# Attention and MLP-mixer kernel: halved fp32 first loads, earlier crossbar transposes, other ring sizes and a new written order

## Chip, cores and metric

The kernel runs on one core of one Trainium2 chip. The metric is device microseconds of one execution; less is better. The time of the kernel before is the median of three runs.

## What is computed

Squared-ReLU attention over 8 batches of 12 heads, 448 positions and 64 channels, and on its result an MLP mixer with a token part and a channel part. Inputs and output are fp32; the kernel computes in bf16 with fp32 sums.

```python
def _attn_ref(q, k, v):                      # 8 x 12 x 448 x 64
    scores = np.matmul(q, k.transpose(0, 1, 3, 2)) / np.sqrt(64)
    attn = np.maximum(scores, 0.0) ** 2 / 448
    return np.matmul(attn, v)

def _moe_ref(x, w_tok1, w_tok2, w_ch1, w_ch2):   # x: 8 x 448 x 768, heads side by side
    h = np.maximum(x.transpose(0, 2, 1) @ w_tok1, 0.0) @ w_tok2     # 448 -> 256 -> 448
    u = x + h.transpose(0, 2, 1)
    return u + np.maximum(u @ w_ch1, 0.0) @ w_ch2                   # 768 -> 1536 -> 768
```

## The kernel before, in words

The attention runs in 24 steps of four heads (three steps for a batch). A step `s` consists of these entries, whose names appear in the written order:

- `ldk`, `ldq`, `ldv`: loads by POOL's queue, which turn fp32 into bf16 on the way. Four buffers each for k and q, three for v. The very first q comes by SP's queue in fp32 (`ldf`) and is turned into bf16 by two `cast` entries.
- `T`: matmul transposes of k and q (56 of 64x64) into a bank, `cp`: copies of the two halves into `kqT`, one of three buffers. From step `QDMA` on the crossbar does this: `ik` and `iq` copy k and q into the only `side` buffer, `xk` and `xq` are DMA transposes on SP's queue from there to `kqT`.
- `S s.c`, c from 0 to 6: scores of 64 keys per head (four 64x64 matmuls of 448 columns), `r`: ReLU of the two banks into an `sq` buffer, on ACT (`:A`) or DVE (`:D`); `q s.c`: the square, on DVE. The `sq` buffers form a ring.
- `V s.c`: the product with v, summed over c; `xe`: eviction into `xT`.
- `X` and `xc`: transpose of x by matmuls and its copy; from step `XDMA` on `xd`, a DMA transpose on SP's queue, stands in their place.
- `t1`, `rt`, `t2`, `u`: the two token products, the ReLU between them, and u = x + h on DVE. `ub`: DMA transposes of u, by batch and 128 channels, into `u_sb`.

The channel part works on rows of 448 positions (one batch). Channel 1: batches 0 and 1 by plain products (`C1`, eviction `c1e`), the others by a scheme with seven products of blocks instead of eight (`Q1` to `Q7`, an entry is 6 matmuls of 224 columns; `m1` to `m4` and `y1` to `y4` are its sums of inputs and weights; `na`, `nb`, `nc` save interim sums; `h11` to `h22` write the result to `r2`). Channel 2 takes pairs of 128-row tiles, again with seven products (`P1` to `P7`, each of six matmuls of 384 columns; `s1` to `s4` and `ws` are the sums), `a`, `b`, `c` and `f11` to `f22` add u and write `out_sb`, `st` stores it. `r2` and `u_sb` are rings of `RING` slots of 128 rows: a channel 1 write waits for the P that read its slot. At `RING` = 8 a batch of 448 rows can lie across the end of the ring, and its write is then split in two.

The order of all entries on all engines is written out in one string, `ORDER`, with a bank number or an engine behind each name; each engine works its own entries strictly in that order. `fill:b*n` puts n matmuls without use on PE.

Of the kernel before, what the change touches and what calls it, by code (L numbers as in the profile page):

```python
# [7 lines left out]
FP32 = mybir.dt.float32  # L8
# [3 lines left out]
XDMA, QDMA = (8, 12)  # L12
# [3 lines left out]
RING = 8  # L16
# [46 lines left out]
ldf ldk0 ldq1 ldk1 ldv0 ident cast0:A cast1:D ldq2 T0.0:0 ldk2 T0.1:1 cp0.0:A ldv1 cp0.1:D ldv2 fill:2*7 S0.0:23  # L63
S0.1:45 S0.3:67 r0.0.0:A r0.0.1:D S0.6:01 ldk3 r0.1.1:A r0.1.0:D S0.4:23 r0.3.1:A ldq3 r0.3.0:D S0.5:54 r0.6.1:A
q0.1:D ldk4 S0.2:76 r0.5.1:A q0.0:D r0.2.1:A fill:1*5 T1.0:14 ldq4 r0.2.0:A r0.6.0:D r0.5.0:A cp1.1:D wt1.0 cp1.0:A
q0.2:D q0.3:D r0.4.1:A fill:6*25 S1.2:67 S1.0:05 r0.4.0:A q0.5:D V0.0:41 wt1.1 r1.0.1:A V0.1 r1.0.0:D V0.2 r1.2.0:A
q0.4:D V0.3 r1.2.1:A wt2 S1.4:32 q0.6:D S1.6:50 V0.4 r1.4.1:A S1.1:67 q1.0:D V0.5 r1.4.0:A r1.1.0:D r1.1.1:A S1.5:23
q1.2:D r1.6.1:A T2.0:67 r1.5.0:A q1.1:D V0.6 r1.5.1:A cp2.1:D ldv3 xe0.1:A cp2.0:D xe0.0:A ldq5 q1.4:D r1.6.0:A
fill:0*22 S2.0:02 S1.3:37 q1.5:D r2.0.1:A X0.0:1 ldk5 V1.0:64 r1.3.1:A r1.3.0:D V1.1 r2.0.0:A q1.6:D X0.1:5 xc0.0:A
S2.1:27 V1.2 q1.3:D S2.3:30 r2.1.0:A r2.1.1:D r2.3.1:A fill:1*6 S2.4:12 V1.3 q2.0:D r2.3.0:A V1.4 r2.4.1:A q2.1:D  # L70
T3.0:70 r2.4.0:A V1.5 q2.3:D cp3.1:A V1.6 cp3.0:D ldv4 q2.4:D xe1.0:A fill:1*9 S3.1:32 S2.5:17 xe1.1:A wc1.0.3
xc0.1:D V2.0:06 r2.5.0:D r2.5.1:A V2.1 S2.2:54 r3.1.1:A wc1.0.1 r3.1.0:D S3.2:71 r2.2.1:A r2.2.0:D T4.0:23 r3.2.1:A
wc1.0.0 q2.5:D S2.6:45 r3.2.0:A X1.1:1 q2.2:D r2.6.1:A wc1.0.2 r2.6.0:A cp4.1:D V2.2 S3.3:75 cp4.0:A xc1.1:D ldk6
V2.3 S3.0:43 r3.3.0:D V2.4 r3.3.1:A ldq6 t1.1.1:1 q2.6:D r3.0.1:A V2.5 q3.3:D r3.0.0:A V2.6 q3.1:D S3.4:27 rt1.1:A
S3.5:53 ldv5 xe2.1:A X1.0:4 xe2.0:D t1.0.1:1 r3.5.1:A wc1.1.1 xc1.0:D t2.1.1:6 r3.5.0:A rt0.1:D t1.0.0:0 r3.4.1:A
q3.0:D wc1.1.2 X2.1:3 r3.4.0:A t2.0.1:4 q3.2:D rt0.0:A S3.6:51 u0.1:D xc2.1:A X2.0:7 T5.0:20 r3.6.1:A r3.6.0:D
wc1.1.0 xc2.0:A V3.0:34 q3.4:D V3.1 cp5.0:A S4.2:15 q3.5:D V3.2 q3.6:D V3.3 r4.2.1:A wc1.1.3 t2.0.0:7 u1.1:D
# [20 lines left out]
C1.1.2:3 q8.1:D xe7.0:A ldk11 xe7.1:A q8.5:D t2.6.1:7 c1e1.2:A ldq11 S9.0:65 u6.1:D V8.1 S8.6:21 r9.0.1:A ldq13 V8.2
r9.0.0:D S9.1:37 r8.6.0:A C1.1.8:5 r8.6.1:D r9.1.1:A ldk13 q9.0:D r9.1.0:A q8.6:D V8.3 ub0.3 c1e1.8:A S9.5:62 V8.4
q9.1:D S9.3:17 V8.5 r9.5.1:A r9.5.0:D S9.4:35 V8.6 r9.3.1:A ub0.4 r9.3.0:D t2.6.0:2 xe8.0:A C1.0.0a:6 q9.5:D xe8.1:A  # L100
r9.4.0:A q9.3:D ub0.1 X7.0:7 r9.4.1:A C1.1.6:1 u6.0:D xc7.0:A q9.4:D ub0.5 ws3.1:D T10.0:40 c1e1.6:A S9.2:35 ws1.1:D
S9.6:27 cp10.1:A ub0.0 C1.1.7:1 r9.2.1:D r9.2.0:A r9.6.1:D r9.6.0:A ub0.2 C1.0.0 q9.2:D cp10.0:A C1.1.11:0 q9.6:D
c1e0.0:A xk12 c1e1.7:D V9.0:53 c1e1.11:A S10.1:72 ws2.1:D V9.1 S10.0:46 r10.1.0:A V9.2 xq12 r10.1.1:D S10.2:10
r10.0.0:A C1.0.8:7 ws4.1:D r10.2.0:A r10.2.1:A xd8 r10.0.1:D t1.7.0:2 c1e0.8:A q10.2:D q10.0:D ub1.0 S10.3:41
rt7.0:A V9.3 q10.1:D S10.5:06 r10.3.0:A V9.4 r10.3.1:D V9.5 r10.5.1:A V10.0:72 ub1.3 s1.0:D V9.6 r10.5.0:A V10.1
T11.0:41 q10.3:D xe9.0:A S10.4:60 xe9.1:A q10.5:D ub1.4 ldk15 C1.1.5:5 cp11.0:A cp11.1:D ldv11 r10.4.1:D r10.4.0:A
V10.2 s2.0:D c1e1.5:A S10.6:31 V10.3 S11.2:40 q10.4:D r10.6.0:A P1.0:6 r10.6.1:A ik13:D r11.2.1:A q10.6:D C1.1.0:5
# [12 lines left out]
r12.0.0:D r12.0.1:A r12.3.0:D nb.2.1:A P2.2:1 q12.0:D c.2:D Q7.2.1 f11.2:D P4.2 xd11 q12.3:D nc.2.1:A iq15:A f22.2:D  # L120
Q5.2.1:2 f21.2:D Q4.2.1 h22.2.1:D st5.0 P3.2 h21.2.1:A xk15 Q2.2.1:5 f12.2:D ub3.1 Q3.2.1 h11.2.1:D S13.0:34
# [710 lines left out]
```

## Time and profile before

| | |
|---|---|
| time, median of 3 runs | 351.92 us (351.30 to 352.77) |
| time of the profiled execution | 351.25 us |
| its span | 349.4 us |
| PE (matmul) busy | 339.6 us, 97% |
| DVE busy | 313.3 us, 90% |
| ACT busy | 223.3 us, 64% |
| POOL busy | 61.8 us, 18% |
| DMA moved | 48.78 MB, mean 140 GB/s |

Busy times come from start and end of instructions, with matmul ends modelled: rows of one engine overlap, so the step from one start to the next, not the length of a row, tells how fast an engine works. `[1.62 <-DMA kq_raw<-in_k_dram]` behind a row means that the engine had stood idle for 1.62 us and that this DMA ended the wait. In the windows, "17.50, 16.75 (x443)" is the length of the stretch, then PE's busy time and its instructions, then the other engines in the order that the heading gives; DMA share is the mean over 16 engines and can exceed 1 where transfers of two queues overlap.

### The profile page before, as it was taken

What the parts mean: (1) busy time and instruction counts of PE and PEld (TensorE: products, weight loads), DVE (VectorE), ACT (ScalarE), POOL (GpSimd) and SP (SyncE); (2) the same over time, 40 slices, a digit from 0 to 9 for tenths busy, and PEclk for the clock granted to TensorE, in tenths of its full rate; (3) what the DMA queues carried; (4) which work ended last, traced back from release to release, by engine and by line L of the source; (5) the groups of instructions that cost most, each with busy time, mean ns of one, the idle gap of its engine ahead of it and who ended that gap; (6) DMA issues with size and microseconds to landing.
All of it is one profiled execution on the core that took longest, in us unless ns stands there. A gap on an engine that the chain in (4) does not pass through costs nothing.

```text
span 349.4 us, 9700 instructions
## 1 busy us (share of the span) xinstructions
PE 339.6 (97%) x3964; PEld 220.0 (63%) x3964; DVE 313.3 (90%) x613; ACT 223.3 (64%) x443; POOL 61.8 (18%) x92
## 2 busy tenths in 40 slices
PE   6999999999999999999999999999999999999993
PEld 2666556555555577668765566666776677888662
DVE  1999999999999997999999999999999985687772
ACT  3999999799995474787655888778655222323100
POOL 8446424044011340004201112101000000000000
PEclk9999999999999999999999999999999999999998
DMA  8999979699999999899986989859853532633235
GB/s 141 201 163 173 208 116 174 114 166 145 150 166 143 192 189 185 139 159 155 187 179 110 195 133 174 168 93 127 145 118 67 104 87 57 127 67 81 57 92 135
DMA packets 93597, 48.78 MB, mean 140 GB/s; under 512 B 68016, under 2 KB 90224, under 8 KB 93552
## 3 DMA queue, kind: packets, MB, share of 16 engines
q1 hardware_dynamic: 68624, 26.30, 41.8%
q0 software_dynamic: 23328, 21.47, 41.6%
q8 instruction: 31, 0.51, 0.6%
q10 hardware_dynamic: 1600, 0.39, 0.5%
q14 instruction: 14, 0.11, 0.1%
HBM read 43.38 MB, written 11.01 MB: 156 GB/s over the span
## 4 chain that ended last, share of the span: by engine, by line
PE 91%; DVE 4%; DMA 2%; issue 1%; ACT 1%; DVEq 0%; POOLq 0%
PE m_ps L701 28%; PE m_ps L619 21%; PE acc_ps L456 9%; PE sc_ps L432 9%; PE m_ps L546 8%; PE t_ps L500 6%; PE h_ps L509 6%; DVE sq L439 2%; DMA kq_raw<-in_k_dram 2%; PE kqT_ps L394 1%; DVE sq L273 1%; PE x_ps L491 1%; ACT sq L271 1%; PE fill_ps L801 0%; DVE kqT L279 0%
## 5 line engine op out<-in xcount | busy, mean ns | idle before, releaser
L271 ACT ACTIVATE sq<-sc_ps 128x448 bf16<-128x448 f32 x247 | 121.8, 580 | 22.3 <-PE sc_ps L432 20.2
L439 DVE TENSOR_TENSOR sq<-sq 128x896 bf16<-128x896 bf16 x168 | 98.5, 614 | 0.3
L432 PE MATMUL sc_ps<-kqT 64*64 64x448 bf16 x672 | 57.6, 356 | 0.5 <-ACT kqT L277 0.2
L456 PE MATMUL acc_ps<-sq,v_raw 64*64 64x448 bf16 x672 | 56.7, 355 | 0.5 <-DVE sq L439 0.5
L277 ACT ACTIVATE snaps<-m_ps 128x448 f32<-128x448 f32 x49 | 27.1, 553 | 46.3 <-PE m_ps L619 23.0
L273 DVE TENSOR_SCALAR sq<-sc_ps 128x448 bf16<-128x448 f32 x89 | 52.9, 615 | 1.2 <-PE sc_ps L432 1.0
L701 PEld LDWEIGHTS <-r_sb 128*128 128x128 bf16 x336 | 31.9, 98 | 22.7 <-issue 4.4
L619 PEld LDWEIGHTS <-wc 128*128 128x128 bf16 x432 | 41.0, 98 | 8.0 <-issue 2.9
L717 DVE TENSOR_TENSOR out_sb<-m_ps,u_sb 128x384 f32<-128x384 f32 x56 | 30.8, 550 | 10.4 <-PE m_ps L701 10.4
L619 PEld LDWEIGHTS <-wy 128*128 128x128 bf16 x324 | 30.4, 98 | 5.7 <-issue 3.1
L701 PEld LDWEIGHTS <-sums 128*128 128x128 bf16 x252 | 24.0, 98 | 15.7 <-issue 2.5
L292 POOL DMA_DIRECT2D v_raw<-in_v_dram x24 | 17.3, 721 | 91.4 <-PE sc_ps L432 48.9
L271 ACT ACTIVATE r_sb<-m_ps 128x448 bf16<-128x448 f32 (+2 forms) x44 | 23.1, 536 | 15.6 <-PE m_ps L619 13.3
L432 PEld LDWEIGHTS <-kqT 64*64 64x64 bf16 x672 | 22.2, 105 | 17.2 <-issue 10.0
L701 PE MATMUL m_ps<-wc_t,r_sb 128*128 128x384 bf16 x168 | 31.9, 326 | 0.6 <-DVE out_sb L717 0.6
L701 PE MATMUL m_ps<-wc,sums 128*128 128x384 bf16 x168 | 31.9, 326 | 0.0
L701 PE MATMUL m_ps<-wc,r_sb 128*128 128x384 bf16 x168 | 31.8, 326 | 0.0
L456 PEld LDWEIGHTS <-v_raw 64*64 64x64 bf16 x672 | 20.3, 105 | 17.1 <-issue 10.8
L546 PE MATMUL m_ps<-uT_sb,wc 128*128 128x448 bf16 x144 | 30.6, 353 | 0.1
L513 DVE TENSOR_TENSOR uT_sb<-h_ps,xT 128x448 bf16<-128x448 f32 x48 | 28.7, 615 | 1.6 <-PE h_ps L509 1.5
L637 DVE CUSTOM_DVE_ANT_0 r_sb<-m_ps,snaps 128x448 bf16<-128x448 f32 x39 | 23.9, 617 | 3.7 <-PE m_ps L619 2.6
L292 POOL DMA_DIRECT2D kq_raw<-in_k_dram x24 | 17.6, 732 | 51.7 <-PE kqT_ps L394 26.7
(62 smaller groups left out, 455.5 us busy)
## 6 DMA issues: line engine op xcount, KB each, us to landing
out_dram<-out_sb SPq DMA_DIRECT2D x52, 192.0 KB, 2.8
kq_raw<-in_k_dram POOLq DMA_DIRECT2D x24, 224.0 KB, 6.8
v_raw<-in_v_dram POOLq DMA_DIRECT2D x24, 224.0 KB, 5.5
kq_raw<-in_q_dram POOLq DMA_DIRECT2D x23, 224.0 KB, 7.5
wc<-in_moe_w_ch_dram POOLq DMA_DIRECT2D x8, 288.0 KB, 9.2
wc<-in_moe_w_ch_dram POOLq DMA_DIRECT2D x4, 576.0 KB, 9.7
u_sb<-uT_sb SPq DMA_TRANSPOSE x60, 3.6
side<-in_q_dram SPq DMA_DIRECT2D x1, 448.0 KB, 3.4
```

The source lines that it names most:

```text
L271: nc.scalar.activation(out, ps, AF.Relu)
L273: nc.vector.tensor_scalar(out=out, in0=ps, scalar1=0.0, scalar2=None, op0=ALU.max)
L277: nc.scalar.activation(out, ps, AF.Copy)
L292: nc.gpsimd.dma_start(out=raws[t][s % NR[t]], in_=rows.rearrange('(e r) x -> r e x', e=2))
L432: nc.tensor.matmul(o.ps[e][64 * half:64 * (half + 1), :S], lhsT=lhsT, rhs=rhs, start=True, stop=True, skip_group_check=True)
L439: sq_ops[s, c] = [add(Op(f'q{s}.{c}', 'DVE', lambda o: nc.vector.tensor_tensor(out=buf, in0=buf, in1=buf, op=ALU.mult), ev))]
L456: nc.tensor.matmul(o.ps[half][64 * e:64 * (e + 1), :S], lhsT=r[rows, e, c * D:(c + 1) * D], rhs=sq[rows, e, :], start=c == 0, stop=c == KC ...
L513: nc.vector.tensor_tensor(out=uTs[bb % 2][:, 2 * i + a, off:off + S].rearrange('n (c p) -> n c p', c=KC), in0=t2.ps[:, :S].rearrange('n (p ...
L546: nc.tensor.matmul(ps[:, :S], lhsT=wc1[:, g, e * 128:(e + 1) * 128], rhs=uT[:, g, off:off + S], start=g == 0, stop=g == CC - 1)
L619: nc.tensor.matmul(banks[into][:, i * SH:(i + 1) * SH], lhsT=lhs[:, g, e * 128:(e + 1) * 128], rhs=rhs[:, g], start=after is None and i == ...
L701: nc.tensor.matmul(banks[into][:, :HN], lhsT=lhs[:, e], rhs=wc2[w][:, e], start=after is None and e == 0, stop=e == EH - 1, skip_group_che ...
L717: nc.vector.tensor_tensor(out=out_, in0=ps, in1=more, op=ALU.add)
```

## The change

- The first k comes in fp32 too, on ACT's queue beside q on SP's. Both come in two halves of 64 partitions, the upper half first; four casts for each half take the place of two. The loads of step 1 by POOL are halved too; `ident` stands behind six POOL loads instead of four. `T0.1` comes ahead of `T0.0`, and each waits for its half alone.
- `XDMA` goes from 8 to 6 and `QDMA` from 12 to 10: `X6`, `X7`, `T10` and `T11` and their copies fall away, `xd6`, `xd7` and the crossings of steps 10 and 11 come in.
- `RING` goes from 8 to 7, so that the ring holds exactly two batches; `sq` gets nine buffers instead of eight, `out_sb` four instead of three.
- Ten warm-up matmuls become eleven, 74 fill matmuls 66.
- `ORDER` is new throughout (1,967 words instead of 1,960). Its first lines are shown.

```diff
-XDMA, QDMA = (8, 12)
+XDMA, QDMA = (6, 10)
-RING = 8
+RING = 7
...
-ldf ldk0 ldq1 ldk1 ldv0 ident cast0:A cast1:D ldq2 T0.0:0 ldk2 T0.1:1 cp0.0:A ldv1 cp0.1:D ldv2 fill:2*7 S0.0:23
...
+ldf.1 ldq1.0 ldf.0 ldq1.1 ldk1.1 ldk1.0 ldv0 castk0.1:A castk1.1:D ldk2 castq0.1:D castq1.1:A ident castk0.0:D castq1.0:A castk1.0:D ldq2 castq0.0:A T0.1:0 T0.0:1 ldv1 cp0.1:A cp0.0:D ldk3 fill:2*7 S0.0:23
...
-    NQ, NSQ, NX, NO = (3, 8, 3, 3)
+    NQ, NSQ, NX, NO = (3, 9, 3, 4)
...
-    q_first = sides[0].rearrange('p a c d -> p (a c d)').bitcast(FP32).rearrange('p (e n) -> p e n', e=2)
+    first = {'q': sides[0].rearrange('p a c d -> p (a c d)'), 'k': sq_all[:, NSQ - 2:].rearrange('p i a n -> p (i a n)')}
+    first = {t: x.bitcast(FP32).rearrange('p (e n) -> p e n', e=2) for t, x in first.items()}
...
+        if s > 1 or t == 'v':
+            loads[s, t] = [add(Op(f'ld{t}{s}', 'POOL', emit, whole=True))]
+        else:
+            loads[s, t] = [add(Op(f'ld{t}{s}.{half}', 'POOL', lambda o, half=half: emit(o, slice(64 * half, 64 * (half + 1))))) for half in range(2)]
...
-    for i in range(10):
+    for i in range(11):
...
     def load_first():
+        for half in (1, 0):
+            part = slice(64 * half, 64 * (half + 1))
+            def emit(o, part=part):
+                for queue, src, dst in ((nc.sync, q, first['q']), (nc.scalar, k, first['k'])):
+                    rows = src[0].rearrange('h (p c) d -> (h p) (c d)', c=KC)[:256].rearrange('(e r) x -> r e x', e=2)
+                    queue.dma_start(out=dst[part], in_=rows[part])
+            ld = add(Op(f'ldf.{half}', 'SP', emit, whole=True))
+            for t in 'kq':
+                for e in range(2):
+                    o = Op(f'cast{t}{e}.{half}', ('DVE', 'ACT')[e], lambda o, t=t, e=e, part=part: copy(o, raws[t][0][part, e], first[t][part, e]), [ld])
+                    loads.setdefault((0, t), []).append(add(o))
...
-        deps = loads[s, 'k'] + loads[s, 'q']
+        deps = [o for t in 'kq' for o in loads[s, t] if n > 1 or o.name.endswith(f'.{halves[0]}')]
...
-    transpose(0, [0])
-    transpose(0, [1])
+    transpose(0, [1])
+    transpose(0, [0])
```

More of the change, by code (lines that the diff above doesn't have):

```diff
@@ L62 @@
 ORDER = """
-ldf ldk0 ldq1 ldk1 ldv0 ident cast0:A cast1:D ldq2 T0.0:0 ldk2 T0.1:1 cp0.0:A ldv1 cp0.1:D ldv2 fill:2*7 S0.0:23
[L64 to L77, printed above, removed]
@@ L98 @@
[L98 to L107, printed above, removed]
@@ L198 @@
-P6.13 f21.12:D st25.0 P5.13:4 b.13:D st26.1.0 P7.13 st25.1 st26.0.0 c.13:D P4.13 f22.13:D st27.1.384 P3.13
-st27.0.384 f21.13:D st27.1.0 f12.13:D st27.0.0 st26.1.384 st26.0.384
+ldf.1 ldq1.0 ldf.0 ldq1.1 ldk1.1 ldk1.0 ldv0 castk0.1:A castk1.1:D ldk2 castq0.1:D castq1.1:A ident castk0.0:D
+castq1.0:A castk1.0:D ldq2 castq0.0:A T0.1:0 T0.0:1 ldv1 cp0.1:A cp0.0:D ldk3 fill:2*7 S0.0:23 ldq3 S0.4:45 S0.5:67
+r0.0.0:A r0.0.1:D S0.1:01 r0.4.1:A ldv2 r0.4.0:D S0.3:23 r0.1.0:A q0.0:D ldk4 S0.2:54 r0.3.1:A q0.4:D r0.2.1:A ldq4
@@ new lines @@
+q8.1:D V7.5 S8.3:57 ub0.3 r8.2.1:A V7.6 r8.2.0:D T9.0:26 r8.3.1:A ldv10 r8.3.0:D C1.0.6:4 xe7.1:A wc2.00 q8.2:D
+cp9.1:A cp9.0:D ldv9 C1.1.7:1 xe7.0:A q8.3:D c1e0.6:A ldq12 q8.4:D ik11:A t1.6.0:7 ws1.1:D ldk12 iq11:A C1.0.8:5
+c1e1.7:D ldq13 ws2.1:D rt6.0:A S8.6:06 y1.1:D c1e0.8:A V8.0:23 S9.1:41 r8.6.1:A V8.1 ws4.1:D S8.5:75 r9.1.1:A V8.2
+xq11 t2.6.1:6 y2.1:D r9.1.0:A C1.1.0:1 r8.5.0:A r8.6.0:D r8.5.1:A xk11 u6.1:D C1.1.8:4 c1e1.0:A q8.6:D q8.5:D ub0.0
+V8.3 q9.1:D c1e1.8:A S9.4:70 V8.4 S9.2:56 r9.4.1:A r9.4.0:D V8.5 ub0.4 S9.0:14 r9.2.1:A r9.2.0:D V8.6 S9.6:07
@@ new lines @@
+nb.5.0:A S22.2:70 ub5.5 S22.1:41 s1.7:D V21.6 r22.2.1:A Q5.5.0:5 q22.0:D r22.1.0:A Q7.5.0 r22.1.1:A s2.7:D ub5.2
+r22.2.0:A s3.7:D t2.18.1:0 nc.5.0:A Q1.5.1:4 s4.7:D ub5.1 q22.1:D t2.18.0:1 na.5.1:A Q2.5.1:7 h22.5.0:D Q4.5.0
+q22.2:D st13.0 Q6.5.1 u18.1:D ub5.4 h21.5.0:A u18.0:D Q3.5.0 h11.5.1:D t2.19.0:0 xe21.1:A st13.1 P1.7:2 h12.5.0:D
+xe21.0:A ub5.0 u19.0:D nb.5.1:A P2.7:1 a.7:D st12.0 P6.7 f11.7:D xd21 S22.3:73 b.7:D S22.4:65 S23.1:01 r22.3.1:A
+r22.3.0:D Q7.5.1 r23.1.1:A r23.1.0:D P7.7 r22.4.1:A q22.3:D nc.5.1:A r22.4.0:A q23.1:D Q5.5.1:3 c.7:D t1.20.0:7
@@ L288, in load, with emit @@
         b, i = divmod(s, GS)
-        def emit(o):
-            rows = src[b].rearrange('h (p c) d -> (h p) (c d)', c=KC)[256 * i:256 * (i + 1)]
-            nc.gpsimd.dma_start(out=raws[t][s % NR[t]], in_=rows.rearrange('(e r) x -> r e x', e=2))
-        loads[s, t] = [add(Op(f'ld{t}{s}', 'POOL', emit, whole=True))]
+        rows = src[b].rearrange('h (p c) d -> (h p) (c d)', c=KC)[256 * i:256 * (i + 1)].rearrange('(e r) x -> r e x', e=2)
+        def emit(o, part=slice(0, 128)):
+            nc.gpsimd.dma_start(out=raws[t][s % NR[t]][part], in_=rows[part])
+        if s > 1 or t == 'v':
+            loads[s, t] = [add(Op(f'ld{t}{s}', 'POOL', emit, whole=True))]
+        else:
+            loads[s, t] = [add(Op(f'ld{t}{s}.{half}', 'POOL', lambda o, half=half: emit(o, slice(64 * half, 64 * (half + 1))))) for half in range(2)]
     def load_wt1():
@@ L349, in load_first @@
     def load_first():
-        rows = q[0].rearrange('h (p c) d -> (h p) (c d)', c=KC)[:256]
-        ld = add(Op('ldf', 'SP', lambda o: nc.sync.dma_start(out=q_first, in_=rows.rearrange('(e r) x -> r e x', e=2)), whole=True))
-        for e in range(2):
-            o = Op(f'cast{e}', ('DVE', 'ACT')[e], lambda o, e=e: copy(o, raws['q'][0][:, e], q_first[:, e]), [ld])
-            loads.setdefault((0, 'q'), []).append(add(o))
-    load(0, 'k')
+        for half in (1, 0):
[9 more added lines that the diff above has]
+                    loads.setdefault((0, t), []).append(add(o))
     load_first()
```

235 lines of the change are left out of this document (125 added, 110 removed).

## Prediction

> **What bounds the kernel now.** I read the page's busy times first, then the same engines by stage (windows cut where the vector engine's idle time changes), then single stretches of the timeline.
>
> ```profile
> span 349.4 us, 9700 instructions
> ## 1 busy us (share of the span) xinstructions
> PE 339.6 (97%) x3964; PEld 220.0 (63%) x3964; DVE 313.3 (90%) x613; ACT 223.3 (64%) x443; POOL 61.8 (18%) x92
> ```
>
> ```profile
> core 0: us, PE busy (x) PEld busy (x) DVE busy (x) ACT busy (x) POOL busy (x), PEclk, DMA share, GB/s
> 9.40:122.50 113.10, 111.60 (x1784) 63.48 (x1777) 112.69 (x212) 99.72 (x202) 36.41 (x52) 1.00 1.08 162
> 122.50:175.00 52.50, 52.50 (x531) 38.02 (x529) 47.87 (x95) 36.78 (x75) 10.04 (x14) 1.00 1.10 169
> 175.00:262.50 87.50, 87.50 (x909) 56.36 (x908) 87.28 (x175) 62.94 (x125) 7.89 (x11) 1.00 0.84 143
> 262.50:287.40 24.90, 24.90 (x236) 17.05 (x234) 23.04 (x47) 8.61 (x18) 0.00 (x0) 1.00 0.39 83
> 287.40:345.40 58.00, 56.72 (x436) 42.07 (x436) 40.59 (x82) 12.48 (x23) 0.00 (x0) 1.00 0.39 89
> ```
>
> PE looks full from end to end, but DVE is full too: from 9.4 to 262.5 us it stands idle only 0.41 + 4.63 + 0.22 = 5.3 us. Which of the two sets the time is told by the steps between starts, since a row's length overlaps the next one.
>
> ```profile
> 103.01 0.55 DVE L717 TENSOR_TENSOR out_sb<-m_ps,u_sb 128x384 f32<-128x384 f32 x1
> 103.47 0.55 DVE L687 TENSOR_TENSOR r_sb<-r_sb 128x768 bf16<-128x768 bf16 x1
> 103.94 0.55 DVE L687 TENSOR_TENSOR sums<-r_sb,sums 128x768 bf16<-128x768 bf16 x1
> 104.41 0.61 DVE L439 TENSOR_TENSOR sq<-sq 128x896 bf16<-128x896 bf16 x1
> 104.94 0.75 DVE L577 TENSOR_TENSOR wc<-wc 128x1152 bf16<-128x1152 bf16 x1
> 105.61 0.61 DVE L439 TENSOR_TENSOR sq<-sq 128x896 bf16<-128x896 bf16 x1
> ...
> 121.58 0.49 DVE L577 TENSOR_TENSOR mt<-uT_sb 128x672 bf16<-128x672 bf16 x1
> 122.00 0.50 DVE L577 TENSOR_TENSOR mt<-uT_sb,mt 128x672 bf16<-128x672 bf16 x1
> ```
>
> So one DVE instruction follows the last after 0.535 us (squarings, and everything that reads 448 columns of a bank), 0.467 (the adds of channel 2, `a b c f` and `s`), 0.67 (weight sums), 0.42 (`m`). The same for the matmul entries:
>
> ```profile
> 234.71 0.36 PE L456 MATMUL acc_ps<-sq,v_raw 64*64 64x448 bf16 x4
> 234.90 0.36 PE L432 MATMUL sc_ps<-kqT 64*64 64x448 bf16 x4
> 235.09 0.36 PE L456 MATMUL acc_ps<-sq,v_raw 64*64 64x448 bf16 x4
> ...
> 289.64 0.54 PE L509 MATMUL h_ps<-wt,r_sb 128*128 128x448 bf16 x2
> 290.02 1.04 PE L500 MATMUL t_ps<-x_sb,wt 128*128 128x256 bf16 x8
> 290.89 1.14 PE L701 MATMUL m_ps<-wc,sums 128*128 128x384 bf16 x6
> 291.87 0.74 PE L619 MATMUL m_ps<-mt,wc 128*128 128x224 bf16 x6
> 292.44 1.14 PE L701 MATMUL m_ps<-wc_t,r_sb 128*128 128x384 bf16 x6
> ```
>
> An S or V entry takes PE 0.19 us, a t2 0.38, a t1 0.87, a P 0.975, a Q 0.575. With these steps I cut the written order where "DVE work done so far plus matmul work still to come" is largest, since neither engine can make that sum shorter. Before, the cut lies at `q23.4`. Done on DVE: 354 entries of 0.535, 88 of 0.467, 16 of 0.67, 16 of 0.42, 11 small ones of about 0.45, and some split writes: 253.4 us. Left on PE: 42 P, 45 Q, 8 t2, 2 t1, 12 S and V: 41.0 + 25.9 + 3.0 + 1.7 + 2.3 = 73.9 us. DVE starts its full run 8.4 us late (next part) and idles 5.3. 253.4 + 8.4 + 5.3 + 73.9 = 341.0; the other 8.4 of 349.4 are PE's gaps in the tail, the last add and the last store. So **DVE bounds the kernel up to about 267 us, PE after it**.
>
> **Part 1: the start.**
>
> ```profile
> 4.19 0.51 DVE L279 CAST kq_raw<-side 128x448 bf16<-128x448 f32 x1 [2.49 <-DMA side<-in_q_dram]
> 8.28 0.62 DVE L279 COPY kqT<-kqT_ps 128x896 bf16<-128x896 bf16 x1 [3.58 <-PE kqT_ps L394]
> 9.40 1.69 DVE L273 TENSOR_SCALAR sq<-sc_ps 128x448 bf16<-128x448 f32 x3 [0.50 <-PE sc_ps L432]
> ```
>
> ```profile
> 7.26 0.98 PE L394 MATMUL kqT_ps<-ident,kq_raw 64*64 64x64 bf16 x56 [1.62 <-DMA kq_raw<-in_k_dram]
> ```
>
> ```profile
> 3.49 0.74 POOL L292 DMA_DIRECT2D v_raw<-in_v_dram  x1
> 4.20 0.25 POOL masks.py:197 MEMSET ident<- 128x128 bf16 x1
> 4.53 0.32 POOL masks.py:199 TENSOR_SCALAR_AFFINE_SELECT ident<-ident 128x128 bf16<-128x128 bf16 x1
> ```
>
> ```profile
> out_dram<-out_sb SPq DMA_DIRECT2D x52, 192.0 KB, 2.8
> kq_raw<-in_k_dram POOLq DMA_DIRECT2D x24, 224.0 KB, 6.8
> v_raw<-in_v_dram POOLq DMA_DIRECT2D x24, 224.0 KB, 5.5
> ...
> side<-in_q_dram SPq DMA_DIRECT2D x1, 448.0 KB, 3.4
> ```
>
> DVE's run begins at 9.40 with 1.04 us of work done (one cast, one copy): an offset of 8.4 us. What PE waits for at 7.26 is k from POOL's queue; q was in by 4.19. Afterwards the first halves of q and k (together the same 448 KB) are in at about 4.2; the second halves lie between that and another 3.4 us later. I take 1.1 us later, 5.3: 256 KB more cost 0.6 us between the two rows above. Two casts in a row on each of two engines make 1.05 us, so the first transposes have their data at 5.3; but the identity, built from 4.20 to 4.85 before, now stands behind six POOL loads instead of four: 4.85 + 2 x 0.71 = 6.3 us, and that ends last. Second half: cast by 6.3, transposed by about 7.2, copied by 7.8. S0 starts at 7.8 and DVE's run at 8.3, against 9.40: **1.1 us gained**. By then DVE has four casts and a copy behind it, 2.5 us, so the offset is 8.3 - 2.5 = 5.8. Bounds: 1.9 gained if the halves cost POOL half the time; 0.9 lost if the second halves need the whole 3.4 us. The added POOL issues put v0 some 0.7 us later and what follows 1.4; the order wants v0 after 6.8 us of DVE work, at 12.6, and 4.2 + 0.7 + 5.5 is 10.4, which hides it. The last half of k1 is issued at about 3.5 and lands 6.8 us later, at 10.3; T1 is wanted after 4.7 us of DVE work, at 10.5. That cover is gone: what k1 is late takes back part of the gain.
>
> The Trainium skill speaks against this part (DMA: Bandwidth & Descriptors, Rules for kernel authors): two transfers to disjoint partition halves serialize, so one should use a single transfer. By that rule the whole loads would be in at the same 5.3, and S0 would start at about 8.0; the sum would be 0.2 us higher. No run so far shows halves.
>
> **Part 2: x and q/k by crossbar from steps 6 and 10.** PE loses T10, T11 (112 small transposes, 1.1 us) and X6, X7 (0.85), and 8 fill matmuls of 0.057 (0.45): 2.4 us in all, less one more warm matmul ahead of the data. All this lies before the cut, beside a full DVE, so I cost it at nothing; if PE were the bound, it would be 2.4 us. ACT loses two copies of x_ps and four of kqT and gains four copies into `side` of the same size: nothing. SP's transposes go from 100 to 94, as the ring of 7 makes 48 of 60 for u_sb. The price that may hide here is a wait, rival 3.
>
> **Part 3: rings.** With 7 slots of 128 rows the ring holds exactly two batches, so no write of channel 1 is split; 15 pairs of DVE writes become single ones, 0.07 us each: 1.0 us of DVE work less, inside the counts below. The other side is one slot less between channel 1's writes and the P that read the slot; the new order pays for it, also in the counts. Score and output rings of 9 and 4: no wait in the trace of before ends on either, so nothing; a loss is excluded, since a larger ring adds no wait.
>
> **Part 4: the new order.** The largest sum now lies at `u18.0`. Done on DVE there: 336 of 0.535, 81 of 0.467, 16 of 0.67, 16 of 0.42, 10 small: 239.4 us, 14.0 less. Left on PE: 49 P, 54 Q, 10 t2, 4 t1, 25 S and V: 47.8 + 31.1 + 3.8 + 3.5 + 4.8 = 91.0 us, 17.1 more. So the order by itself is 3.1 us worse. What it gives back is DVE's idle time. Before, nearly all of it (4.6 us) lies in 122.5 to 175. There the order puts 61.9 us of matmuls beside 60 us of DVE work (between 100 and 160 us of DVE work done), and PE needs 64.6 for it. The new order has 57.9 beside the same 60; by the same ratio PE needs 60.4, so 0.4 to 1 us of idle time is left. I take 1.6 in all (0.41 + 0.22 + 1.0), with 0.6 and 5.3 as the ends. The tail grows from 74 to 91 us of matmuls, so I let its gaps and end grow from 8.4 to 9.4.
>
> **Sum.** 239.4 + 5.8 + 1.6 + 91.0 + 9.4 = 347.2 against 349.4: 2.2 us less, in pieces: offset -2.6, DVE work -14.0, idle -3.7, matmuls left +17.1, tail +1.0. The profiled run was 351.25, 1.85 over its span; the median is 351.92. Taking the difference to the median gives **349.7 us**. Measurement tells about 0.5% (1.8 us) from no change, so faster means under 350.2, slower over 353.7.
>
> **Rivals.** (1) *PE is the bound throughout*, as its full columns and the chain of waits say. Then Part 2's 2.4 us and the start's 1.1 count and the order costs nothing: 348.4. Against it stand DVE's steps without a gap for 113 us. (2) *DVE's idle time does not shrink*, because with the shorter ring PE is again behind when P and Q are wanted: 5.3 instead of 1.6, 353.4. For it: the stretch with idle time in before is just where P and Q begin. (3) *The crossing stalls ACT*, the slower end.
>
> ```profile
> DMA to landing us min/median/max: 3.0/4.1/9.7
> ```
>
> That is the landing of the crossbar's q/k transposes. There is one `side` buffer, so `ik11` waits on ACT until `xk10` has landed. The order gives it 5.8 us of DVE work and `iq11` 4.9; before, the first such pair had 8.7 and 9.0. This stage has ACT busy 99.72 of 113.10 us and the DMA share at 1.08. Behind `ik11` on ACT stand the evictions of scores, and DVE's squarings wait for those. At 4.1 nothing happens; from 4.9 on every microsecond counts, up to 9.7 - 4.9 = 4.8, which gives 354.5, and from 4.0 the kernel is slower than before by the bound. Later pairs with little room (3.5 us at step 16) could add to it.
> The Trainium skill (Advanced Engine Details and Errata, X-Bar Transpose) has transposing DMAs as fast as plain ones, at 350 to 400 GB/s. For these 229 KB that is, as an estimate, 0.7 us on the wire, and rival 3 would fall away; the measured 4.1 and 9.7 do not support it.
>
> **How the numbers follow.** Forecast 0.46, own range 347 to 352 (the ends of start and idle time): 0.36 of it faster, 0.10 the same. Rival 1 0.20, faster. Rival 2 0.16: 0.09 the same, 0.07 slower. Rival 3 0.18: 0.03 the same, 0.15 slower. Faster 0.56, same 0.22, slower 0.22. Low end: forecast with the best start, idle 0.6 and no longer tail, 349.7 - 0.8 - 1.0 - 1.0 = 346.9, and the start of rival 1 with it, 346. High end: rival 3, 354.5.
>
> **What would show it.** Right: first score evictions on DVE near 8.3; DVE without idle time from there to about 247 us, except 1 to 2 us; after it PE full, with 91 us of matmuls; first P near 105. Wrong: a stretch of several us of DVE idle time ending on ACT `sq`, behind a `side` copy that waits for a kqT transpose (rival 3); idle time around the first P and Q that ends on PE (rival 2); DVE idle all over while PE ends earlier (rival 1); first transposes later than 7.3.

## The result: 361.27 us instead of 351.61, slower by 2.6%

The changed kernel takes 361.27 us (median of 4 runs, 359.78 to 363.13), the kernel before beside it 351.61 (351.27 to 352.77): a ratio of 1.0264, 95% interval 1.0223 to 1.0306. The forecast was 349.7, its range ended at 354.5, and neither the sign nor the range held. The profiled execution took 362.22 us. (Some executions fall in a slower state; the ratios leave them out, and nothing here rests on the trace of `e17_late9_sp_whole`, which fell in it.) From the page of the changed kernel: busy times, and the lines of DVE, the granted clock and the DMA engines in 40 slices of 9.0 us.

```profile
span 360.5 us, 9396 instructions
## 1 busy us (share of the span) xinstructions
PE 342.4 (95%) x3829; PEld 225.5 (63%) x3829; DVE 311.9 (87%) x598; ACT 223.5 (62%) x444; POOL 61.4 (17%) x93
...
DVE  2798999999999289999999999979997974695693
...
PEclk9699999999999789999999999999999999999999
DMA  8999989969999959989989998986970364057227
```

DVE has less to do, as forecast, and the span is 11.1 us longer. Two places stand out: slice 2 (9 to 18 us), where the clock falls to 6 tenths, and slice 14 (117 to 126 us), where DVE falls to 2. The same kernel by stage:

```profile
core 0: us, PE busy (x) PEld busy (x) DVE busy (x) ACT busy (x) POOL busy (x), PEclk, DMA share, GB/s
...
11.40:20.00 8.60, 8.15 (x149) 5.70 (x142) 7.93 (x15) 7.45 (x17) 2.37 (x4) 0.76 1.29 202
20.00:111.00 91.00, 88.18 (x1375) 50.76 (x1375) 89.92 (x168) 82.92 (x170) 29.05 (x43) 1.00 1.06 163
111.00:128.00 17.00, 11.41 (x60) 6.43 (x58) 9.42 (x19) 2.44 (x4) 4.24 (x7) 0.81 1.27 164
128.00:264.00 136.00, 135.19 (x1409) 92.46 (x1408) 131.72 (x255) 98.14 (x196) 16.11 (x23) 1.00 0.99 151
```

From 11.4 to 264 us DVE's idle time is 0.67 + 1.08 + 7.58 + 4.28 = 13.6 us, where 1.6 was forecast. In the stage with most of it, 111 to 128 us, only the DMA engines are fully used (share 1.27). Who waits for whom there (timeline rows of DVE, PE, POOL and SP's queue, then the chain of waits):

```profile
126.20 0.62 DVE L524 TENSOR_TENSOR uT_sb<-h_ps,xT 128x448 bf16<-128x448 f32 x1 [6.40 <-PE h_ps L520]
```

```profile
123.53 1.89 PE L511 MATMUL t_ps<-x_sb,wt 128*128 128x256 bf16 x8 [5.59 <-DMA x_sb<-xT]
```

```profile
109.59 2.11 POOL L294 DMA_DIRECT2D v_raw<-in_v_dram  x3 [11.23 <-PE acc_ps L467]
111.75 1.42 POOL L294 DMA_DIRECT2D kq_raw<-in_q_dram  x2
113.14 0.72 POOL L294 DMA_DIRECT2D kq_raw<-in_k_dram  x1
114.43 1.43 POOL L294 DMA_DIRECT2D kq_raw<-in_k_dram  x2 [0.56 <-issue]
```

```profile
103.75 3.43 SPq L425 DMA_TRANSPOSE kqT<-side  x2
107.24 3.88 SPq L536 DMA_TRANSPOSE u_sb<-uT_sb  x3
111.21 1.36 SPq L490 DMA_TRANSPOSE x_sb<-xT  x1
```

```profile
111.21 12.27 DMA x_sb<-xT
```

PE stands at `t1.9`, which wants x of step 9. Its crossbar transpose was issued at 111.21 us, behind five others on SP's queue, and took 12.27 us to land, among eight loads that POOL put out from 109.6 to 115.9 us.

At the start, the second halves are late (DVE's rows; the cast at 7.27 is that of k's lower half):

```profile
4.71 0.70 DVE L281 CAST kq_raw<-sq 64x448 bf16<-64x448 f32 x1 [3.00 <-DMA sq<-in_k_dram]
5.61 0.39 DVE L281 CAST kq_raw<-side 64x448 bf16<-64x448 f32 x1 [0.20 <-DMA side<-in_q_dram]
7.27 0.78 DVE L281 CAST kq_raw<-sq 64x448 bf16<-64x448 f32 x2 [1.27 <-DMA sq<-in_k_dram]
9.85 0.62 DVE L281 COPY kqT<-kqT_ps 128x896 bf16<-128x896 bf16 x1 [1.80 <-PE kqT_ps L405]
11.39 1.16 DVE L275 TENSOR_SCALAR sq<-sc_ps 128x448 bf16<-128x448 f32 x2 [0.92 <-PE sc_ps L443]
```

DVE's run begins at 11.39 us, not 8.3.

### The profile page after: what moved, and what is told of

The parts are those of the page before. It is cut to its first block, busy times and chain, and to the rows that moved or that the text cites. A ratio compares the mean times of both kernels' runs of the same rounds, so it can differ in the third digit from the quotient of the medians.

```text
span 360.5 us, 9396 instructions
## 1 busy us (share of the span) xinstructions
PE 342.4 (95%) x3829; PEld 225.5 (63%) x3829; DVE 311.9 (87%) x598; ACT 223.5 (62%) x444; POOL 61.4 (17%) x93
## 4 chain that ended last, share of the span: by engine, by line
PE 68%; DVE 11%; DMA 9%; ACT 6%; issue 3%; SPq 0%; ACTq 0%; DVEq 0%
PE m_ps L712 23%; PE m_ps L630 19%; PE sc_ps L443 6%; PE acc_ps L467 6%; PE m_ps L557 5%; ACT sq L273 4%; DVE sq L450 4%; DMA kqT<-side 4%; PE t_ps L511 4%; PE h_ps L520 4%; DMA x_sb<-xT 3%; DVE sq L275 3%; DMA side<-in_q_dram 2%; DVE uT_sb L524 2%; PE fill_ps L812 1%
## 5 line engine op out<-in xcount | busy, mean ns | idle before, releaser
L273 ACT ACTIVATE sq<-sc_ps 128x448 bf16<-128x448 f32 x245 | 118.5, 569 | 27.0 <-PE sc_ps L443 26.0
L450 DVE TENSOR_TENSOR sq<-sq 128x896 bf16<-128x896 bf16 x168 | 97.3, 611 | 0.2
L443 PE MATMUL sc_ps<-kqT 64*64 64x448 bf16 x672 | 61.1, 364 | 1.5 <-DVE kqT L281 0.6
L275 DVE TENSOR_SCALAR sq<-sc_ps 128x448 bf16<-128x448 f32 x91 | 53.8, 612 | 1.6 <-PE sc_ps L443 1.4
L279 ACT ACTIVATE snaps<-m_ps 128x448 f32<-128x448 f32 x53 | 29.3, 556 | 40.6 <-PE m_ps L630 19.0
L648 DVE CUSTOM_DVE_ANT_0 r_sb<-m_ps,snaps 128x448 bf16<-128x448 f32 x54 | 32.7, 616 | 9.9 <-PE m_ps L630 7.1
L443 PEld LDWEIGHTS <-kqT 64*64 64x64 bf16 x672 | 25.4, 107 | 21.8 <-issue 13.1
L294 POOL DMA_DIRECT2D v_raw<-in_v_dram x24 | 17.1, 714 | 105.2 <-PE acc_ps L467 86.4
L273 ACT ACTIVATE r_sb<-m_ps 128x448 bf16<-128x448 f32 x38 | 20.7, 550 | 18.5 <-PE m_ps L630 12.4
L511 PE MATMUL t_ps<-x_sb,wt 128*128 128x256 bf16 (+1 forms) x216 | 26.2, 266 | 5.6 <-DMA x_sb<-xT 5.6
L467 PEld LDWEIGHTS <-v_raw 64*64 64x64 bf16 x672 | 21.2, 106 | 15.7 <-issue 9.4
```

What stands on the lines that cost most here:

```text
L273: nc.scalar.activation(out, ps, AF.Relu)
L275: nc.vector.tensor_scalar(out=out, in0=ps, scalar1=0.0, scalar2=None, op0=ALU.max)
L443: nc.tensor.matmul(o.ps[e][64 * half:64 * (half + 1), :S], lhsT=lhsT, rhs=rhs, start=True, stop=True, skip_group_check=True)
L450: sq_ops[s, c] = [add(Op(f'q{s}.{c}', 'DVE', lambda o: nc.vector.tensor_tensor(out=buf, in0=buf, in1=buf, op=ALU.mult), ev))]
L467: nc.tensor.matmul(o.ps[half][64 * e:64 * (e + 1), :S], lhsT=r[rows, e, c * D:(c + 1) * D], rhs=sq[rows, e, :], start=c == 0, stop=c == KC ...
L511: nc.tensor.matmul(o.ps[:, j, :], lhsT=wt1[:, c, j * 128:(j + 1) * 128], rhs=x_sb[:, p0:p1, c, :], start=c == 0, stop=c == 3)
```

## Experiments

Ratios are to the kernel before, measured in the same series. Kernels with the new order scatter more from run to run (some 2 us to either side, the kernel before about 1), so places and waits are read from the traces, and the times only decide what is larger than that. How far one kernel is ahead of another at some point is read from the starts of the same write of u (DVE's row `uT_sb<-h_ps,xT`) in both traces. In the diffs, entries of the written order stand for the place they have there.

### The start alone, in the old order

`e14_before_half` puts Part 1 as it is into the kernel before; `e13_before_whole` does the same without halves:

```diff
-        for half in (1, 0):
-            part = slice(64 * half, 64 * (half + 1))
+        for half in (0,):
+            part = slice(0, 128)
...
-ldf.1 ldq1.0 ldf.0 ldq1.1 ldk1.1 ldk1.0 ldv0 (8 casts) T0.1:0 T0.0:1
+ldf.0 ldq1 ldk1 ldv0 ident (4 casts) T0.0:0 T0.1:1
```

> The kernel before with Part 1 alone (first k and q in fp32 by SP's and ACT's queues in halves of 64 partitions, step 1 in halves by POOL), everything else old. If Part 1 is what the changed kernel loses before 100 us: first scores' eviction on DVE at 11 to 11.6 instead of 9.4 us with 2.5 instead of 1.0 us done, half clock from about 8.8 to 15.6 us, x1 evicted 3 to 4 us later, and, as the old order has no stall that takes this up, 353.5 to 355.5. By the prediction's own step (first scores at 8.3): 350.5 to 351.

> The kernel before with the first k and q in fp32 by SP's and ACT's queues as in Part 1, but each in one transfer of 128 partitions, with step 1 whole as before. If it is the halves that make the start late (second halves in after 4.8 and 5.7 us at the median, a whole q after 3.4): both are in by 4.5 to 5.5 us, transposed at 6 to 7, first scores' eviction on DVE at 8.0 to 8.8, clock full throughout, 350.5 to 351.5. If two transfers of 448 KB side by side take as long as the halves: first transposes at 7.5 to 8, 351.5 to 353.

With halves the ratio is 1.0051 (1.0014 to 1.0089), whole 0.9976 (0.9951 to 1.0001). First evictions of scores on DVE, first with halves, then whole:

```profile
10.82 1.69 DVE L273 TENSOR_SCALAR sq<-sc_ps 128x448 bf16<-128x448 f32 x3 [0.72 <-PE sc_ps L441]
```

```profile
8.47 1.69 DVE L272 TENSOR_SCALAR sq<-sc_ps 128x448 bf16<-128x448 f32 x3 [0.50 <-PE sc_ps L437]
```

So k by a hardware queue does what the prediction wanted of it (8.47 against its 8.3). The halves, with the casts and loads that they add, undo it. A whole q and k land side by side in 4.4 and 4.7 us; the halves take 4.4 and 5.6 us at the median, and the kernel waits for the second pair. The rule of the Trainium skill (DMA: Bandwidth & Descriptors, Rules for kernel authors) that disjoint partition halves serialize and one transfer should be used pointed the right way; the price was larger than the 0.2 us that I gave it.

### The start, inside the changed kernel

`e5_whole` makes the same edit in the changed kernel, `e3_start` gives it the old start, and `e4_fill` keeps PE busy between the halves:

```diff
-T0.1:0 T0.0:1
+T0.1:0 fill:2*18 T0.0:1
...
-    for i in range(11):
+    for i in range(12):
```

> The changed kernel with 18 idle matmuls on zeros between the two first groups of transposes and one more ahead of the first; nothing else. Theory (the granted clock falls to half from 8.8 to 15.6 us because PE does too little from 5.4 to 8.8): the granted clock stays at 1.0 there, the first scores start at the same 10.6 us, T1 and V0 come 1 to 1.5 us earlier, and the time is 1 to 2 us shorter, 359.5 to 360.3. Rival (what counts at the start is the late data alone): 361 to 361.6, clock or no clock.

> The changed kernel with the first loads, casts and transposes of the kernel before (q whole in fp32 by SP, k whole with conversion by POOL, one cast per engine, step 1 whole), everything from the first scores on as in the changed kernel. Theory: DVE's run begins at 9.4 instead of 11.4 us with one us of work done instead of 2.5, so the offset of 8.9 goes back to 8.4 at least; the granted clock stays at 1.0 from 6 us on instead of half from 8.8 to 15.6, which brings another 1 to 3 us by the marker at 25 us (x1 evicted at 25.1 instead of 28.8). The later stall at 111 to 128 us stays: 357.5 to 359.5. Rival (whatever is won at the start is lost again to PE or to the loads): 360.5 to 362.5.

> The changed kernel with the same one edit: first k and q by the same two queues, but whole, step 1 whole; order, rings and crossbar as changed. The start as in the kernel before with whole transfers (eviction at 8.0 to 8.8, x1 evicted at 25 to 26 instead of 28.8). What is won up to 100 us is 3 us; theory D lets the stall near 120 us take a part of it back, as it did with the old start: 357 to 360.5. If the start is worth its 3 us to the end: 357.5 to 358.5.

The clock from 8.8 to 15.6 us, changed kernel and then with the fill matmuls:

```profile
8.80:15.60 6.80, 6.15 (x113) 4.85 (x114) 4.48 (x9) 5.28 (x11) 4.84 (x7) 0.50 1.26 203
```

```profile
8.80:15.60 6.80, 5.74 (x142) 4.20 (x146) 5.35 (x10) 5.88 (x12) 4.44 (x7) 1.00 1.26 203
```

The clock is mended, and x of step 1 is evicted at 27.4 instead of 28.8 us (26.0 with the old start, 25.2 with whole loads). In the times nothing of it is left: ratios 1.0336 (1.0283 to 1.0389) with fill, 1.0270 (1.0229 to 1.0310) with the old start, 1.0220 (1.0149 to 1.0291) with whole loads, against 1.0264. The gains forecast for the old start (357.5 to 359.5) and for the fill (359.5 to 360.3) did not come, and the fill came out above its rival's range too.

In the traces the lead goes in more than one place. From 38 to 107 us the old start is 3.4 us ahead of the changed kernel, the fill matmuls 2.4. At the stall near 120 us they lose 0.7 and 1.4 (DVE's longest idle time there is 6.40 us in the changed kernel, 6.90 and 7.81 in these two), and near 200 us another 1.4 and 2.4, where DVE waits for ACT. At `u18.0` the old start is still 2.0 us ahead, which the scatter of the times covers; the fill is 1.3 behind. Whole loads lose 3.2 of their 3.6 us by 36 us already, at PE:

```profile
28.44 0.48 PE L399 MATMUL kqT_ps<-ident,kq_raw 64*64 64x64 bf16 x19 [2.40 <-issue]
```

The changed kernel stops at the same instruction for 0.89 us. Behind the longer stop the granted clock is 0.50 from 28 to 34 us, where the changed kernel has 1.00. So this run says little about the stall.

### What the stall near 120 us waits for

`e12_no_loads` takes DMA work away; the other four only move it, or move what wants it.

```diff
+            if f'{t}{s}' in 'v11 v12 v13 k14 q14 k15 k16 q17'.split():
+                return
             nc.gpsimd.dma_start(out=raws[t][s % NR[t]][part], in_=rows[part])
```

> The changed kernel without eight of POOL's loads of 224 KB (v11, v12, v13, k14, q14, k15, k16, q17, those of the burst at 109.6 to 115.9 us; the steps compute on what the buffers held before). Theory D and theory A (burst) agree here: some 8 loads of about 1.9 us less DMA work, the transpose of x9 lands after 3 to 5 us, the stall goes, 352 to 355. If what holds x9 up is SP's own pace (1.26 us and more per transpose), it is still issued at 111 us and t1.9 waits 1 to 2 us: 355 to 357. Theory C: 359 to 362.

Ratio 1.0097 (1.0052 to 1.0142); the profiled execution took 354.52 us, 7.7 less than that of the changed kernel. By the two ratios the gain is 1.7%, some 6 us. The same stage, 105 to 128 us, before (changed kernel) and after the loads are left out:

```profile
105.00:128.00 23.00, 17.41 (x139) 9.92 (x128) 15.42 (x30) 8.44 (x17) 5.65 (x8) 0.86 1.12 157
```

```profile
105.00:128.00 23.00, 23.00 (x217) 14.73 (x210) 23.00 (x47) 12.77 (x26) 0.00 (x0) 1.00 0.69 112
```

DVE and PE run through, although x9's transpose was issued later than before (112.35 instead of 111.21 us): the transposes of x now land in 3.3 us at the median instead of 10.7. SP's pace is not the reason; the loads beside the transposes are.

`e1_loads` moves loads on POOL's queue to where their buffers come free:

```diff
-T9.0 ldv10 wc2.00 ldv9 ldq12 ldk12 ... P1.0 ldv13 ldv11 ldv12 ldq17 ldq14 ldk16 ldk15 ldk14
+V6.6 ldv9 ... T9.0 ldk12 ldq12 wc2.00 ldv10 ... V8.6 ldv11 ... ldq15 ldk14 ldq14 ldk15 ... V9.6 ldv12 V10.6 ldv13
```

> The changed kernel with nothing moved but loads on POOL's queue: each stands where its buffer comes free and none waits at the head while others behind it could go (the load of v9 behind the products of v6, v11 behind those of v8, v12 behind v9, v13 behind v10; k12 and q12 ahead of v10; k14, q14, k15 behind q15; k16 and q17 later). Theory A (the 12 us of DVE idle time at 111 to 128 us come from eight software loads that go out at once from 109.6 to 115.9 us, while the crossbar transpose of x9 stands behind them: it lands after 12.3 us): x9 lands after 4 to 5 us, idle time there under 2 us, the second period of half clock (121.4 to 128.3) gone, 352 to 354 us. Theory B (the crossbar transpose is late because SP issues it late, at 111.2 us, behind five other transposes): landing shorter but t1.9 still waits 2 to 4 us, 356 to 358. Theory C (the new order or the shorter ring costs the time, whatever the loads do): 360 to 362.

Theory A (a burst at the wrong moment, and nothing else) falls: ratio 1.0378 (1.0309 to 1.0446), and DVE still idles 5.23 us, to 126.2; all three theories had forecast a shorter time. The loads went out earlier, and the transposes before x9's paid instead: those of q and k took 7.3 us at the median between 70 and 123 us, not 4.6, and x9's was issued at 114.36.

`e2_sp` moves `ub1.2 ub1.4 ub1.5` behind `xd9` on SP's queue, `e15_sp_start` adds the old start to it, and `e16_late9` moves `t1.9`:

```diff
-t1.9.0:0 b.1:D ... m1.2:D rt9.0:A xd10 P7.1 ... P3.0 ... P4.1 ... P2.0:6 ... V11.0:30
+b.1:D ... m1.2:D xd10 P7.1 ... P3.0 ... P4.1 ... P2.0:6 t1.9.0:2 ... V11.0:30 rt9.0:A
```

> The changed kernel with three of SP's transposes of u_sb (ub1.2, ub1.4, ub1.5) moved from ahead of the transpose of x9 to behind it, loads as they are. Theory A (burst of loads): x9 is issued 3 to 4 us earlier, near 107.5 us, ahead of most of the burst, and lands in 4 to 6 us; the stall of 6.4 us goes and the time is 353 to 356. Theory B (SP's queue): the same 353 to 356; it is this kernel and the one with moved loads together that part them: only under B does this one gain more than that one. Theory C (order or ring): 360 to 362.

> The changed kernel with the old start and the three transposes of u_sb moved behind that of x9 (the two edits tried singly). If the two gains add (start 3 us, stall 3 to 4 us): 353 to 356. If the DMA engines pace both, the transposes of u_sb that now come later are wanted by the first adds of channel 2 at the same time as before, the stall there grows by what the start gained: 356 to 360.

> The changed kernel with one matmul group moved in the order: t1.9, which waits for the crossbar transpose of x9, stands four products of channel 2 later (behind P2.0, 4.3 us of matmuls), with its eviction. If only x9 is late and everything else behind it is there (rival: a lack of slack in the order at one place): PE's wait of 5.6 us falls to 1 to 2 us, the time by 4 to 5 us, 356 to 357.5. Theory D (the DMA engines are behind with all that is wanted near 120 us): the products run, but their first adds then wait for transposes of u_sb, or the scores of step 12 for those of its keys and queries; what is won is 1 to 3 us, 358 to 360.

Ratios 1.0254 (1.0196 to 1.0313), 1.0233 (1.0169 to 1.0297) and 1.0364 (1.0292 to 1.0437). In all three `t1.9` no longer waits; in `e2_sp`, where x9's transpose goes out at 106.6 us, ahead of the loads, it lands in 3.3. DVE's rows, in the order of the names:

```profile
122.96 0.56 DVE L725 TENSOR_TENSOR out_sb<-m_ps,u_sb 128x384 f32<-128x384 f32 x1 [3.66 <-DMA u_sb<-uT_sb]
```

```profile
124.00 0.56 DVE L714 TENSOR_TENSOR out_sb<-m_ps,u_sb 128x384 f32<-128x384 f32 x1 [5.70 <-DMA u_sb<-uT_sb]
```

```profile
125.74 0.56 DVE L725 TENSOR_TENSOR out_sb<-m_ps,u_sb 128x384 f32<-128x384 f32 x1 [6.40 <-DMA u_sb<-uT_sb]
```

The third is the clearest. With x9 out of the way DVE idles the same 6.40 us, half a microsecond earlier, now for a transpose of u that is 9.85 us under way. In the times none of the three shows the gain that was forecast for it. It isn't one transfer that the order wants too early: the transposes that go out beside those loads or behind them are late here, whichever they are. Of the edits that only move something, `e2_sp` shortened the idle time most, by 2.8 us; leaving loads out removed it.

`e17_late9_sp_whole` puts whole loads, the moved u transposes and the later `t1.9` together:

> The changed kernel with the three edits together that each took something away: first k and q whole on the two hardware queues, three transposes of u_sb behind that of x9, t1.9 four products later. If the waits are single places that can be mended one by one: 352.5 to 355. Theory D: the start's 3 us are lost again by 36 us and at 120 us, 357 to 360.

Ratio 1.0221 (1.0132 to 1.0310), from two executions: the three edits do not add up, which is what theory D expected.

### Parts 2 to 4 apart

`e7_pe_again` undoes Part 2 in the changed kernel, `e10_pe_start` Parts 1 and 2, and `e8_before_x` puts Part 2 alone into the old order. In each the entries had to be placed by hand, which is a change of its own.

```diff
-XDMA, QDMA = (6, 10)
+XDMA, QDMA = (8, 12)
...
-xd6 xd7 ik10 iq10 xk10 xq10 ik11 iq11 xk11 xq11
+xe7.1:A X6.0 ... c1e0.6:A X7.0 ... c1e1.0:A T10.0 ... xe8.0:A T11.0   (and their copies)
```

> The changed kernel with Part 2 undone: x of steps 6 and 7 and queries and keys of steps 10 and 11 are transposed on PE again, six crossbar transposes fewer before the first products of channel 2; order, rings and start otherwise as changed. Theory D (the DMA engines are full up to about 125 us, and the new order asks for more DMA work by then than they can do: six transposes of about 1.3 us each are 8 us of it): the transpose of x9 is issued and lands some 6 to 8 us earlier, idle time of DVE at 111 to 128 us falls from 7.7 to under 2, no second period of half clock, 352.5 to 355. Theory C (order or ring, whatever the DMA engines do): 359.5 to 362.

> The changed kernel with Parts 1 and 2 undone: old start, PE transposes up to steps 7 and 11; what is left of the change is the order and the rings. Theory D: no stall at 111 to 128 us and DVE's run from 9.3 us on, so the sum of the prediction for Part 4 alone holds: 239.4 of DVE work, 8.4 offset, 2 to 4 idle, 91 left on PE and 7 to 9 of tail, a time of 349 to 353. Theory C: 358 to 361.

> The kernel before with Part 2 alone: x from step 6 and queries and keys from step 10 by crossbar, in the old order, with the old start and the old rings. Theory D: the six transposes take 8 us of DMA time in the same full stretch, but the old order wants x9 some 15 us of matmuls after its transpose instead of 10 and the first products of channel 2 later, so a part of it is covered: 352 to 357. If crossbar transposes cost nothing here, as the prediction had it: 351 to 352.5.

Ratios 1.0318 (1.0226 to 1.0410), 1.0140 (1.0099 to 1.0182) and 1.0406 (1.0300 to 1.0513); theory D's times were too low for all three. In `e7_pe_again` and `e10_pe_start` the stall near 120 us is gone. DVE's row for `e10_pe_start` has no idle time there (busy 28.00 of 28.00 us), beside the same eight loads:

```profile
100.00:128.00 28.00, 28.00 (x262) 17.07 (x260) 28.00 (x55) 16.00 (x33) 5.63 (x8) 1.00 1.25 160
```

The starts of the same three writes of u, in us, show where time is lost and won:

| | 1st | 2nd | 3rd |
|---|---|---|---|
| changed kernel | 74.83 | 103.91 | 137.68 |
| `e3_start` (Part 1 undone) | 71.45 | 100.54 | 135.47 |
| `e7_pe_again` (Part 2 undone) | 75.48 | 108.68 | 134.48 |
| `e10_pe_start` (both undone) | 71.77 | 104.96 | 130.76 |

From the first to the second, the kernels with PE transposes lose 4.1 us against the changed one, because the evictions of the scores wait for PE between 80 and 100 us; from the second to the third, over the stall, they win 8.0. That is not only because they come later: in `e10_pe_start` x of step 9 is evicted 1.1 us later than in the changed kernel (106.8 against 105.6), but its transpose is issued 1.5 us earlier, at 109.75, 0.9 us ahead of the first of the loads, and lands in 3.1 us. With the old start alone (`e3_start`) it is issued 2.3 us behind the first of them and lands in 12.1. So the order and the rings, with PE's transposes placed like this, do not make the stall; with Part 2's crossbar transposes ahead of x9's on SP's queue they do. By the third mark Part 2 costs 8.0 - 4.1 = 3.9 us.

`e7_pe_again` then lost 4.95 us at another place, which no theory had (DVE's row and the chain of waits):

```profile
199.15 0.63 DVE L447 TENSOR_TENSOR sq<-sq 128x896 bf16<-128x896 bf16 x1 [4.95 <-ACT sq L270]
```

```profile
184.25 13.41 DMA kqT<-side
```

A crossbar transpose of keys under way for 13.41 us, the next copy into `side` waiting for it on ACT, the evictions behind that copy, DVE behind them: rival 3, at a later step. In `e8_before_x` the same chain holds DVE up for 7.82 us near 104 us, and for 3.94 us at 74 us behind a load of k; with my placing of the crossings that kernel tells what a crossing can cost, not what Part 2 costs at its best.

`e10_pe_start` leaves the order and the rings. Its profiled execution took 357.10 us with a span of 355.2: a run from 9.2 us on, and 9.3 us of idle time, 3.1 of it between 80 and 100 us, where my placing has a share, and 5.2 after 128 us. By the prediction's terms Part 4 alone (-14.0 - 3.7 + 17.1 + 1.0) was worth +0.4 us; here, with the rings and this placing, it costs about 5 (1.4% of 352).

No kernel tried is clearly faster than the one before; `e13_before_whole` comes nearest, at 0.9976.

## Why the prediction was wrong

Its sum, term by term, in the changed kernel: DVE work 239.4 as counted; offset 8.9 (11.39 less 2.5 of work done) instead of 5.8; idle time 13.6 instead of 1.6; from `u18.0` (at 263.2 us) to the end 97.3 instead of 91.0 + 9.4 = 100.4. That makes 359.2; the other 1.3 of the 360.5 are DVE steps a little longer than counted.

- **Idle time (Part 4), the step that failed: 1.6 us in the sum, 13.6 in the trace.** It was found by setting PE's matmuls against DVE's work in one stage, 122 to 175 us. There the forecast of 1.0 was about right (1.3 us from 128 to 175, beside the end of the stall). The idle time came elsewhere, 1.8 us before 111 us, 7.7 near 120 and 2.8 after 175, and most of it from a third resource. By its sign the stall looks like rival 2 (idle time near the first P that ends on PE), but PE itself waited for a transfer. The prediction quoted DMA shares of 1.08 and 1.10 and used them for rival 3 only. Counted along the written orders in DVE work (an estimate, with the prediction's steps), the new one first uses x of step 9 after about 107 us, the old one after about 113; by 107 us the new order has used 8 crossbar transposes of x, q and k and some 40 loads, the old one 3 and as many loads. Up to 123 us the DMA engines were as full on the mean in both kernels, and moved as much:

```profile
0.00:123.00 123.00, 1.00 1.06 161
```

```profile
0.00:123.00 123.00, 0.97 1.09 166
```

The first row is the kernel before, the second the changed one (clock, DMA share, GB/s). These are means: in the changed kernel the share is 0.46 from 70 to 75 us and 0.73 from 75 to 80. "DMA work done" was a third line under which the cut had to be looked for, beside DVE and PE. In the trace without eight loads the 7.7 us (6.40 + 1.30 of the gap) are gone, and so they are with Part 2's transposes back on PE; the move of `t1.9` shows that the wait belongs to no single transfer. The other 4 us of unforeseen idle time are short waits, mostly for PE, that no run took apart.

- **Part 1, wrong by its sign.** The step "The second halves lie between that and another 3.4 us later. I take 1.1 us later" failed: the cast of the lower half of k began 2.56 us after that of the upper (7.27 against 4.71), and PE then ran at half clock from 8.8 to 15.6 us. DVE's run began 2.0 us late in the changed kernel (11.39 against 9.40) and 1.4 late in the old order (10.82), where 1.1 of gain was forecast. The bound of "0.9 lost" was itself too small: 3.4 us in place of 1.1 is 2.3 later, and makes 1.2 lost. In the old order the part costs 0.5% (0.1 to 0.9%). In the changed kernel its price to the end isn't shown: the old start keeps 2.0 us of its lead in the trace and none in the times.
- **Part 2, "I cost it at nothing".** Costed on the engine that it left, and not on the queue that it joined: on SP's queue five more transposes of x, q and k stand ahead of x9's than in the old order. Undoing it (`e7_pe_again`, `e10_pe_start`) cost 4.1 us on PE and took 8.0 away at the stall.
- **Rival 3** was the nearest rival by mechanism, at the wrong step. At 10 to 11 the landing stayed at 4.6 us (median, 70 to 123 us), and none of ACT's copies into `side` waited there; the late landing hit x9 first, and keys or queries issued near 185 us in several of the edited kernels (9.98 us with fill, 13.41 in `e7_pe_again`).
- **Right:** less DVE work before the cut and more matmuls after it, and a tail no longer than forecast (97.3 us from `u18.0` to the end, against 100.4).

What stays open: how the 7.7 us would divide between order and crossbar, since both raise the demand before 120 us, either eight loads or six transposes less were enough to end the stall, and no kernel here undid one part without moving something else; and what Part 2 costs in the old order at its best. Part 3 was not tried alone.

## What to carry to other kernels

An order can be bounded by the transfers too: count, along the order, what each entry needs by DMA, and look for the place where "DMA work wanted so far" runs ahead of what the engines moved by that time in the profile. Where the mean DMA share is at 1 for a hundred microseconds, a wait that ends on a transfer need not be mended by moving that transfer or its user: here the next transfer was late in its place. Test it by leaving loads out, and see whether the wait moves or goes. And look at how a queue's transfers lie to a burst on another: here x9's transpose landed in 3.1 to 3.3 us ahead of the loads and in 12.1 to 12.3 behind the first of them.

## What the runs showed of the hardware

- The landing of a crossbar transpose of 229 KB (128 x 896 bf16) depends on what runs beside it: 3.3 us at the median without the loads (`e12_no_loads`, 105 to 128 us), 9.1 and 12.3 us in the changed kernel, where eight loads went out from 109.6 to 115.9 us, up to 13.41 for keys (`e7_pe_again`). The Trainium skill (DMA: Bandwidth & Descriptors, Rules for kernel authors) says that spreading DMAs over issuing engines gives no bandwidth, since all run on the same 16 engines and interleave. These runs agree as far as they go: transposes on SP's queue land late beside loads on POOL's.
- PE's granted clock fell to 0.50 from 8.8 to 15.6 us after a stretch with only small transposes and gaps (PE busy 1.63 of 3.40 us before it), and to 0.51 from 121.4 to 128.3 us, in the stall. Filling the first stretch with idle matmuls kept it at 1.00. The Trainium skill (TensorE: Matmul & The Clock Gate, What's actually happening) gives a free-running window of about 3.4 us, after which an idle PE is halved; two such windows are 6.8 us, an estimate from that figure, and 6.8 and 6.9 were seen.
- PE stopped for 2.40 us in the middle of 56 small transposes with nothing to wait for (`<-issue`), in `e5_whole`, with a DMA share of 1.15 and more around it, and 0.89 at the same instruction in the changed kernel. That it waited for its instructions is an inference; one transfer of an instruction queue (0.02 MB) was under way at 26 us, as the stop began, but the view does not tell for which engine. The Trainium skill (Runtime: NRT & Kernel Launch, Instruction fetch mechanics) has instructions fetched in blocks through a DMA queue of the sequencer's own, at a cost that is mostly hidden; if the inference holds, it was not hidden here.
